# Hash attention and SwiGLU on one core: both query rows of a head pair in sequence, then one stretch of feed-forward work

## The chip, the core and the metric

The kernel runs on one core of one Trainium2 chip. The metric is the device time of one execution in microseconds (us), the median of several runs. A profile of one execution goes with it: the engines are PE (TensorE matmul), PEld (its weight loads), DVE (VectorE), ACT (ScalarE), POOL (GpSimd) and SP (SyncE, which issues transfers).

## The reference

Two blocks follow each other. The attention works on 4 batches of 8 heads, 768 positions of 64 dimensions, with a mask that lets a query see only the keys of its own hash bucket:

```python
q_bits = (np.einsum('bhsd,dk->bhsk', q, proj) > 0)      # 6 bits, the same for k
mask = q_bucket[:, :, :, None] == k_bucket[:, :, None, :]
scores = np.where(mask, scale * np.matmul(q, k.transpose(0, 1, 3, 2)), -1e9)
attn = np.exp(scores - max);  attn = attn / (attn.sum + 1e-9)
x = np.matmul(attn, v)      # heads side by side: 3072 tokens x 512
g = x @ w_gate              # 512 x 1536
out = (g * sigmoid(g) * (x @ w_val)) @ w_out            # 1536 x 512
```

All matrix products are in fp32.

## The kernel before

**Attention.** Heads are taken in pairs, 16 in all (`n` = 0 to 15, four to a batch). For each pair the 768 queries fall into two rows (`half` 0 and 1) of 384; each row runs over 6 blocks of 128 keys (`NCH`). A row's steps are

- `score(u)` (L484): for each key block, fp32 products of q and k for both heads and a bf16 product of hash signs that adds the mask (`sc`, L494); ScalarE takes the exponential into one of six weight buffers (L497);
- `add(u)` (L518): VectorE adds the row's weights of the six key blocks into `acc`, one operation of 128 x 768 for each of the blocks 1 to 5 (L523, L527);
- `attend(u)` (L500): weights times v (`av`, L509), then ScalarE copies the result to `xT`;
- after the second row `total(n)` (L529): four PE products with ones sum `acc` of both rows over the partitions (`sum`, L540), VectorE takes the reciprocal (L548), and eight transfers on SP's queue spread it; `norm` (L558, L560) multiplies `xT` by it later, when `finish(waiting)` comes.

The next pair is prepared by `front(n + 1)` (L388): from pair 5 on two transposes on VectorE (L457), then four small PE products for the hash (`hps`, L412), four sign operations on ScalarE (L417), a transfer that spreads q's signs (L429) and two VectorE operations for k's (L426). `load` (L108) fetches q, k and v of the pair after it, on SP's queue.

**Feed-forward.** A batch whose four pairs are done is pushed by `push_ffn` (L832) as a list of `atoms`, small steps written in PE order: six groups `both(i)` of up products (`up`), then three groups `chunk(i)` of down products (`po`). They use Strassen's scheme, so operands are combined by VectorE (`plus`, L597) before or after the products. In batches 1 to 3 a group of up products is nested: `deeper` (L703) splits two products again, and `weigh` (L696) forms their combined weights, four VectorE operations on 128 x 128. `weigh(0)` of a group can be made ahead by `look_ahead()` (L585), which the last step of the group before calls too. The operands made once for each batch, 16 VectorE operations, stand in the list `first` and are issued by `finish(first)`. A group's steps have sizes that add up to 14. The weights come back from DRAM in pieces: `bring` (L322) issues a transfer on POOL's queue once the product that read the old piece is done.

**Order.** The program order is written out by hand in the loop at L862. From pair 4 on (`gating`) a stretch of feed-forward steps of the batch before follows each row: the loop adds 14 (pairs 4 to 7) or 15.75 (pairs 8 to 15) to `credit` and takes steps until the credit is used up, but only stops at the end of a group. `chores`, one for each unit of size, weave the next pair's preparation into the stretch: in the first row's stretch the two transposes, in the second row's stretch the hash and what follows from it. PE takes its matmuls in this order, and each engine its own instructions.

PSUM has seven rotating banks for all of `sc`, `up`, `po`, `hps` and `sum`, and one for `av`.

Of the kernel before, what the change touches and what calls it, by code (L numbers as in the profile page):

```python
# [18 lines left out]
def kernel(  # L19
# [20 lines left out]
    NP = H // 2  # L40
# [32 lines left out]
    pairs = [(b, pr) for b in range(B) for pr in range(NP)]  # L73
    raws = {}

    def fetch(n, name, queue, half=None):
        b, pr = pairs[n]
        if name == "v":
            t = raws["v", n] = raw.tile([P, 2, NCH, D], FP32, tag="vraw", name="vraw")
            queue.dma_start(  # L80
                t.rearrange("p h c d -> p h (c d)"),
                v[b, 2 * pr : 2 * pr + 2].rearrange("h (p c) d -> p h (c d)", c=NCH),
            )
            return
        src = q if name == "q" else k
        if not half:
            raws[name, n] = raw.tile([P, NCH, 2, D], FP32, tag=name + "raw", name=name + "raw",
                                     bufs=1)
        t = raws[name, n]
        if n <= NP:  # L90
            cs = slice(None) if half is None else slice(half * CH, (half + 1) * CH)
            for h in range(2):
                queue.dma_start(t[:, cs, h, :],
                                src[b, 2 * pr + h].rearrange("(p c) d -> p c d", c=NCH)[:, cs, :])
            return


        blocks = t.rearrange("p c a b -> p (c a b)").rearrange(
            "p (c a d) -> p c a d", a=P // BLOCK, d=BLOCK)
        for h in range(2):  # L100
            for x in range(D // BLOCK):
                at = h * D + x * BLOCK
                queue.dma_start(
                    blocks[at : at + BLOCK],
                    src[b, 2 * pr + h][:, x * BLOCK : (x + 1) * BLOCK].rearrange(
                        "(a p c) d -> p c a d", c=NCH, p=BLOCK))

    def load(n, names):  # L108
        if n < len(pairs):
            for name in names:  # L110
                fetch(n, name, nc.sync)
# [189 lines left out]
    def scale_ahead():  # L301
        scale_to(min(progress["piece"] + 4, progress["scaled"] + 1))
# [70 lines left out]
    def prepare_on(n):  # L373
        for _ in range(n):
            next(preparing, None)
# [108 lines left out]
    def score(u):  # L484
        n, half, c = units[u]
        qs = slice(half * HQ, (half + 1) * HQ)
        ks = slice(c * P, (c + 1) * P)
        sc = [bank("sc")[:, 0:HQ] for _ in range(2)]
        for x, start in ((T, True), (bits, False)):
            if u < 2 and not start:  # L490
                prepare_pair(1)
            for h in range(2):
                rows = slice(h * D, (h + 1) * D)
                nc.tensor.matmul(sc[h], x["k", n][rows, ks], x["q", n][rows, qs],  # L494
                                 start=start, stop=not start)
        for h in range(2):
            nc.scalar.activation(weights(u)[:, h, 0:HQ], sc[h], AF.Exp,  # L497
                                 scale=SCALE * (OFF / 2 if n <= NP else 1.0))
# [19 lines left out]
    def add(u):  # L518
        n, half, c = units[u]
        a = weights(u)  # L520
        if c == 1:
            acc[n, half] = att.tile([P, 2, HQ], FP32, tag="acc", name="acc")
            nc.vector.scalar_tensor_tensor(out=acc[n, half], in0=weights(u - 1)[:, :, 0:HQ],  # L523
                                           scalar=S * EPS / P, in1=a[:, :, 0:HQ],
                                           op0=ALU.add, op1=ALU.add)
        elif c > 1:
            nc.vector.tensor_tensor(acc[n, half], acc[n, half], a[:, :, 0:HQ], op=ALU.add)  # L527

    def total(n):  # L529

        b, pr = pairs[n]

        ps = av_ps.tile([P, 512], FP32, tag="av", name="sum") if b == 0 else bank("sum")
        t = [acc.pop((n, half)) for half in range(2)]
        for h in range(2):
            for half in range(2):
                g = (2 * h + half) * BLOCK
                nc.tensor.matmul(ps[g : g + BLOCK, 0:HQ], ones, t[half][:, h, :],  # L540
                                 start=True, stop=True)
        if b == 0:
            space = wo.rearrange("p f m -> p (f m)")
            space = space[:, n % 2 * 3 * HQ : (n % 2 + 1) * 3 * HQ].rearrange("p (x q) -> p x q", q=HQ)
            r, t = space[:, 2, :], space[:, 0:2, :]
        else:
            r, t = t[1][:, 0, :], t[0]
        nc.vector.reciprocal(r, ps[:, 0:HQ])  # L548
        for half in range(2):
            for h in range(2):  # L550
                g = (2 * h + half) * BLOCK
                for at in (h * D, h * D + BLOCK):
                    nc.sync.dma_start(t[at : at + BLOCK, half, :], r[g : g + BLOCK, :])
        waiting.append(lambda: norm(n, t))
        if pr == NP - 1:
            push_ffn(b)
# [24 lines left out]
    def finish(todo):  # L581
        while todo:
            todo.pop(0)()

    def look_ahead():  # L585

        if atoms:
            finish(getattr(atoms[0][1], "ahead", []))
# [265 lines left out]
    def prepare_pair(count):  # L854
        for _ in range(count):
            rest.extend(f for f in steps.pop(0)() or [] if f)
# [4 lines left out]
    credit = 0.0  # L861
    for u in range(0, N, NCH):  # L862
        n, half, _ = units[u]
        gating = u >= LATE
        if u == MOVE:
            progress["late"] = True
            for t in late_ring:
                nc.gpsimd.memset(t[:, :, HQ:AW], 1.0)
        for c in range(NCH):
            score(u + c)  # L870
            if u + c == 2 or not gating and half == 1 and c == 2:
                prepare_pair(1)
            if c == 1 and half == 0 and 0 < n <= NP:
                total(n - 1)
            if c:
                add(u + c)
        if n >= 2 * NP:
            look_ahead()
        if (n < NP and half == 1) or u == LATE or (n >= 2 * NP and half == 0):
            finish(waiting)  # L880
        finish(rest)
        if not gating and half == 0:
            steps = front(n + 1)
        if not gating and half == 0 and u > 0:
            prepare_pair(2)
        for _ in range(1 if u else 2):
            scale_ahead()
        for c in range(NCH):
            attend(u + c)
        if not gating:  # L890
            scale_ahead()
        if half == 1:
            load(n + 2, "qkv" if n + 2 > NP else "v")
        elif not gating:
            prepare_pair(2 if u > 0 else 4)
            if n + 2 <= NP:
                load(n + 2, "qk")
        finish(first)
        prepare_on(0 if u == LATE else 4)
        chores = []  # L900
        if half == 1 and n >= NP:
            total(n)
            if n + 1 < len(pairs):
                chores = [None] + steps.pop(0)()
        prepare_on(0 if LATE - NCH <= u <= LATE else 3 if gating or not half else 1)
        if not gating:
            continue
        if n + 1 < len(pairs) and half == 0:
            steps = front(n + 1)
            chores = [None, steps.pop(0), None, steps.pop(0)]  # L910

        credit += 14 if n < 2 * NP else 15.75
        end = True
        part = 0
        while atoms and (credit > 0 or not end):
            size, atom, end = atoms.pop(0)
            credit -= size
            atom()
            part += size
            if n < 2 * NP and part >= 11 or u + NCH == N and part >= 6:  # L920
                finish(waiting)
                if u + NCH == N:
                    finish([first.pop(0) for _ in range(min(2, len(first)))])
            if 5 < part < 14 if u == LATE else part < (9 if u < LATE + 3 * NCH else 11):
                prepare_on(size)
            if 6 < part < 11 or u == LATE and part > 10:
                scale_ahead()
            for _ in range(size):
                if chores:
                    step = chores.pop(0)  # L930
                    chores.extend(step and step() or [])
        while chores:
            step = chores.pop(0)
            chores.extend(step and step() or [])
# [34 lines left out]
```

## Time and profile before

| what | value |
|---|---|
| time, median of 3 runs | 986.15 us (985.97 to 986.3) |
| the profiled execution | 985.97 us |
| its span, first to last instruction | 983.9 us |
| granted TensorE clock | 0.999 |
| first scores of pair 8 | 323.87 us from the span's start |
| one row, first `sc` to the end of `av` | 9.09 us |
| one group of up products (nested) | 17.68 us |
| one group of down products | 18.33 us |
| end of the last `sum` (pair 15) | 784.2 us |

Busy time is the share of the span in which an engine executes; matmuls are pipelined, so starts, and not durations, tell what one costs. The chain that ended last is followed back from the last instruction, at each step to what released it or to the instruction before it on its engine. In a timeline each line is a start, a duration (of all the merged instructions), the engine, its line in the kernel, the operation, output<-inputs and a count; idle time before it and what ended it stand in brackets.

From 323.87 us on, two groups follow the first row of pairs 8 and 12 (the last down group of one batch and the first up group of the next), and one group follows each other row of pairs 8 to 14. In each of those stretches ScalarE and VectorE are busy for part of the time only: in the up group from 461.35 to 479.03 us VectorE for 11.27 us of 17.68.

### The profile page before, as it was taken

To read this page: it belongs to the slowest core of one execution; us is meant where nothing else is said; L and a number is where in the kernel's file an instruction comes from. 1 tells how busy PE (TensorE), PEld (TensorE's weight loads), DVE (VectorE), ACT (ScalarE), POOL (GpSimd) and SP (SyncE) were. 2 spreads that over 40 slices of the span, in tenths; PEclk is the share of its full clock that TensorE was granted. 3 is DMA by queue.
4 is the path that set the end of the run, shared out by engine and by line. 5 is a ranking of instruction groups with operands and counts; after the bars stand their busy time and mean duration, and the time that the engine had idled before them with its cause. 6 is when DMAs were issued, how large, how long until landed. Compare 5 with 4: busy or idle time off the path is not lost.

```text
span 983.9 us, 13575 instructions
## 1 busy us (share of the span) xinstructions
PE 977.7 (99%) x4813; PEld 624.2 (63%) x4813; DVE 669.6 (68%) x1276; ACT 408.2 (41%) x921; POOL 127.2 (13%) x248
## 2 busy tenths in 40 slices
PE   9999999999999999999999999999999999999998
PEld 4444555555576776556567776666556687666787
DVE  5899888888974647768775465676767444767721
ACT  6999555566413225444342224335443212333200
POOL 3232232241100011101110001110101000121000
PEclk9999999999999999999999999999999999999999
DMA  7787685976303043323432204343122011333000
GB/s 231 219 259 220 153 260 171 242 271 172 110 17 78 17 100 106 86 85 93 109 93 45 66 17 113 93 98 103 58 67 76 22 38 65 107 102 110 18 28 33
DMA packets 119987, 107.02 MB, mean 109 GB/s; under 512 B 90032, under 2 KB 104848, under 8 KB 119920
## 3 DMA queue, kind: packets, MB, share of 16 engines
q0 software_dynamic: 18336, 73.29, 23.0%
q1 hardware_dynamic: 100784, 32.67, 14.2%
q8 instruction: 38, 0.62, 0.3%
q10 hardware_dynamic: 800, 0.20, 0.1%
q14 instruction: 29, 0.24, 0.1%
HBM read 81.79 MB, written 17.30 MB: 101 GB/s over the span
## 4 chain that ended last, share of the span: by engine, by line
PE 95%; DVE 2%; ACT 2%; issue 1%; DVEq 0%; ACTq 0%
PE up L593 42%; PE po L593 22%; PE sc L494 15%; PE av L509 12%; PE sum L540 1%; PE hps L412 1%; PE tps L396 1%; ACT A L497 1%; ACT kb L417 1%; DVE room L368 0%; PE idle L134 0%; DVE acc L527 0%; ACT room L497 0%; DVE hid L575 0%; DVE c L571 0%
## 5 line engine op out<-in xcount | busy, mean ns | idle before, releaser
L593 PE MATMUL up<-xT,room 128*128 128x384 f32 (+1 forms) x732 | 243.0, 465 | 0.0
L593 PEld LDWEIGHTS up<-xT,room 128*128 128x128 f32 x732 | 134.8, 190 | 73.3 <-issue 9.8
L593 PE MATMUL up<-xc,room 128*128 128x384 f32 (+1 forms) x540 | 176.9, 455 | 0.0
L327 POOL DMA_DIRECT2D room<-ram x144 | 77.6, 542 | 671.0 <-PE up L593 654.3
L494 PE MATMUL sc<-qT,kT 64*128 64x384 f32 x768 | 159.5, 493 | 0.0
L527 DVE TENSOR_TENSOR acc<-acc,A 128x768 f32<-128x768 f32 x128 | 122.6, 958 | 15.7 <-ACT A L497 2.9
L597 DVE TENSOR_TENSOR c<-c,up 128x192 f32<-128x192 f32 (+1 forms) x198 | 78.8, 406 | 76.7 <-PE up L593 72.3
L593 PEld LDWEIGHTS up<-xc,room 128*128 128x128 f32 x540 | 99.3, 190 | 43.8 <-DVE c L597 1.1
L570 ACT ACTIVATE th<-c 128x384 f32<-128x384 f32 x90 | 47.0, 522 | 156.4 <-DVE c L571 87.6
L497 ACT ACTIVATE A<-sc 128x384 f32<-128x384 f32 x256 | 104.0, 527 | 0.6 <-PE sc L494 0.5
L815 ACT COPY words<-po 128x256 f32<-128x256 f32 x48 | 17.9, 372 | 198.5 <-PE po L593 179.6
L494 PEld LDWEIGHTS sc<-qT,kT 64*128 64x128 f32 x768 | 66.1, 186 | 53.6 <-issue 41.2
L597 DVE TENSOR_TENSOR hid<-hid,up 128x192 f32<-128x192 f32 (+1 forms) x162 | 67.6, 418 | 42.8 <-PE up L593 41.0
L509 PE MATMUL av<-A,vraw 128*64 128x384 f32 (+1 forms) x512 | 88.2, 486 | 0.0
L597 DVE TENSOR_TENSOR words<-words,po 128x256 f32<-128x256 f32 x36 | 15.1, 420 | 95.8 <-PE po L593 95.8
L679 ACT COPY c<-up 128x384 f32<-128x384 f32 x72 | 34.4, 478 | 81.6 <-PE up L593 81.6
L593 PE MATMUL po<-wo,room 128*128 128x256 f32 x288 | 66.3, 379 | 0.5 <-DVE room L597 0.5
L593 PE MATMUL po<-wo,hid 128*128 128x256 f32 x288 | 66.7, 382 | 0.0
L593 PE MATMUL po<-room,hid 128*128 128x256 f32 x288 | 66.2, 379 | 0.5 <-ACT words L815 0.5
L509 PEld LDWEIGHTS av<-A,vraw 128*64 128x64 f32 x512 | 36.7, 137 | 46.0 <-issue 44.4
L494 PE MATMUL sc<-qb,kb 64*128 64x384 bf16 x384 | 63.2, 323 | 0.5 <-DVE kb L426 0.5
L593 PEld LDWEIGHTS po<-wo,hid 128*128 128x128 f32 x288 | 54.1, 190 | 12.1 <-issue 4.9
(137 smaller groups left out, 1166.1 us busy)
## 6 DMA issues: line engine op xcount, KB each, us to landing
room<-ram POOLq DMA_DIRECT2D x96, 384.0 KB, 3.7
vraw<-in_v_dram SPq DMA_DIRECT2D x16, 384.0 KB, 3.3
ram<-room POOLq DMA_DIRECT2D x12, 512.0 KB, 5.0
room<-ram POOLq DMA_DIRECT2D x48, 128.0 KB, 3.5
out_dram<-words SPq DMA_DIRECT2D x48, 128.0 KB, 1.7
room<-in_moe_w_out_dram POOLq DMA_DIRECT2D x10, 512.0 KB, 6.6
qraw<-in_q_dram SPq DMA_DIRECT2D x48, 96.0 KB, 3.0
hid<-in_moe_w_gate_dram POOLq DMA_DIRECT2D x9, 512.0 KB, 6.9
```

What stands on the lines that cost most here:

```text
L327: nc.gpsimd.dma_start(places[k % 2][:, PARTS[go], :], ram[k % NG][:, PARTS[go], :])
L396: nc.tensor.transpose(ps[:, i * P : (i + 1) * P], raws[name, n][:, half * CH + i, :, :].rearrange("p h d -> p (h d)"), ident)
L412: nc.tensor.matmul(tile_[i * BLOCK : (i + 1) * BLOCK, 0:HQ], hash_w, T[name, n][:, half * HQ : (half + 1) * HQ], start=True, stop=True)
L494: nc.tensor.matmul(sc[h], x["k", n][rows, ks], x["q", n][rows, qs], start=start, stop=not start)
L497: nc.scalar.activation(weights(u)[:, h, 0:HQ], sc[h], AF.Exp, scale=SCALE * (OFF / 2 if n <= NP else 1.0))
L509: nc.tensor.matmul(ps[h * D : (h + 1) * D, 0:width], raws["v", n][:, h, c, :], a[:, h, 0:width], start=c == 0, stop=c == NCH - 1)
L527: nc.vector.tensor_tensor(acc[n, half], acc[n, half], a[:, :, 0:HQ], op=ALU.add)
L570: nc.scalar.activation(th, g, AF.Tanh, scale=0.5)
L593: nc.tensor.matmul(ps, a, x, start=start and i == 0, stop=i == len(pairs_) - 1, skip_group_check=True)
L597: nc.vector.tensor_tensor(o, a, b, op=op)
L679: nc.scalar.copy(tile_of(g, spot), c)
L815: nc.scalar.copy(o, c)
```

## The change

For the pairs of the third and fourth batch (`whole`, n >= 8) both rows run one after the other, and one stretch of feed-forward steps follows the second, with a credit of 31.5 in place of twice 15.75. The number of steps taken by the end of a pair is the same. In that stretch stand, in order: the reciprocal and spreading of the pair's sums; at unit 6 and 8 the two transposes, at unit 9 the loads for pair n + 2 (before: behind the second row, ahead of the sum), and at unit 15 the hash, followed by the signs. `look_ahead()` is called only after the second row's scores. `finish(waiting)`, the normalisation of the pair before, and `finish(first)` stay behind the first row. Nothing is changed for pairs 0 to 7, and no instruction is added or removed other than in the order.

```diff
+        whole = n >= 2 * NP
...
-        if n >= 2 * NP:
+        if whole and half:
             look_ahead()
...
-        if half == 1:
+        if whole:
+            pass
+        elif half == 1:
             load(n + 2, "qkv" if n + 2 > NP else "v")
...
         if half == 1 and n >= NP:
             total(n)
-            if n + 1 < len(pairs):
+            if n + 1 < len(pairs) and not whole:
                 chores = [None] + steps.pop(0)()
...
-        if not gating:
+        if not gating or whole and not half:
             continue
-        if n + 1 < len(pairs) and half == 0:
+        if n + 1 < len(pairs) and whole:
+            turn_q, turn_k, hashes = front(n + 1)
+            chores = 5 * [None] + [turn_q, None, turn_k, lambda: load(n + 2, "qkv")]
+            chores += 5 * [None] + [hashes]
+        elif n + 1 < len(pairs) and half == 0:
             steps = front(n + 1)
             chores = [None, steps.pop(0), None, steps.pop(0)]
 
-        credit += 14 if n < 2 * NP else 15.75
+        credit += 31.5 if whole else 14
```

By the order of groups this gives: pair 8, the last down group of batch 0 and up groups 1 and 2 of batch 1; pair 9, up groups 3 and 4; pair 10, up groups 5 and 6; pair 11, down groups 1 and 2; and the same again for pairs 12 to 15. The last down group of batch 2 and all of batch 3 follow after pair 15, as before.

## The prediction

> **What bounds the kernel now.** I read the page's engine rows first, then the chain that ended last in order of time, then single engines' timelines around one pair of heads, then the engines' instruction orders in the two programs.
>
> ```profile
> PE 977.7 (99%) x4813; PEld 624.2 (63%) x4813; DVE 669.6 (68%) x1276; ACT 408.2 (41%) x921; POOL 127.2 (13%) x248
> PE 95%; DVE 2%; ACT 2%; issue 1%; DVEq 0%; ACTq 0%
> ```
>
> The chain names TensorE (PE) for 95% of the span, so only what lengthens or shortens PE's own sequence counts. In the changed region (pairs 8 to 15, from 323.9 us) the chain holds nothing but PE pieces, end to end:
>
> ```profile
> 452.27 5.04 PE sc L494 x36
> 457.31 4.04 PE av L509 x24
> 461.35 17.68 PE up L593 x68
> 479.03 5.04 PE sc L494 x36
> 484.08 4.02 PE av L509 x24
> 488.10 0.94 PE sum L540 x8
> 489.04 0.65 PE hps L412 x8
> 489.69 17.68 PE up L593 x68
> 507.37 5.04 PE sc L494 x36
> ```
>
> That is pair 10: first row (sc, av), a group of up products, second row, the sum of the weights, the hash of the next pair, a second group. The change issues the same matmuls in another order. It can save only switches between kinds of matmul and short waits, and it can lose wherever VectorE (DVE), 68% busy, now comes late. One short wait shows already: sum takes 0.94 here but 0.78 in pair 11 (543.85), with hps 0.65 in both. VectorE's last addition before this sum starts at 484.00 in a run of four lasting 4.14, so it ends at 488.14, while the sum's matmuls start at 488.03: **0.16 us of waiting**, in pairs 8, 9, 10, 12, 13 and 14.
>
> **Part 1, the switches.** Streaming costs come from starts that follow each other without a change of kind: 0.3225 us for a 384-wide fp32 matmul instruction (four in 1.29), 0.1613 for 192-wide, half of it for two that share the array. What a start lies behind these is the switch. The rows of one switch after another, in PE's timeline:
>
> ```profile
> 477.58 1.45 PE L593 MATMUL up<-xT,room 128*128 128x384 f32 x4
> 478.96 0.92 PE L494 MATMUL sc<-qT,kT 64*128 64x384 f32 x4
> 479.71 0.33 PE L494 MATMUL sc<-qb,kb 64*128 64x384 bf16 x2
> 479.87 0.81 PE L494 MATMUL sc<-qT,kT 64*128 64x384 f32 x4
> 480.52 0.33 PE L494 MATMUL sc<-qb,kb 64*128 64x384 bf16 x2
> ```
>
> 477.58 + 1.29 = 478.87, and sc starts at 478.96: 0.09. The first four sc take 0.75, the next four 0.65: 0.10 more. So up to sc costs 0.19. In the same way: av to up 0.10, and 0.11 in the first up run (3.01 from start to start where 2.90 is streaming), 0.21; sum to po with no hash between (783.45 to 784.23, 0.645 streaming) 0.13 + 0.11 = 0.24; sum, hps, po (543.78 to 545.20, 1.29 streaming) again 0.24; av to sc (first heads, 97.06) 0.10 + 0.10 = 0.20. A hash in the middle of other work shows at 89.64: 0.10 to enter, 0.78 for 0.645 of streaming, then the slower first run.
>
> Old order per pair: up to sc 0.19, av to up 0.21, sum, hps, up 0.24: 0.64. New order: av to sc 0.20, sum to up 0.24, and the hash, which now stands after the second group's first step, 0.09 + 0.13 + 0.11 = 0.33: 0.77. That is +0.13 in each of pairs 8 to 14, about +0.9. Pair 15 has no hash and saves 0.20. The waits at the sum go in six pairs: -1.0. **Part 1 comes to -0.3 us**, between -1.7 (a hash inside the group costs only its streaming and the leaving switch is free) and +0.9 (it costs 0.17 more each time, twice the leaving row).
>
> The Trainium skill, TensorEngine Tiling, Key Properties, says that a change of tiling mode drains the array. The starts above agree that a change of kind costs time. Counted by that rule, the new order has one change more per pair with a hash and one fewer in pair 15, six more in all; at an estimated 0.1 to 0.2 each that would be +0.6 to +1.2 before the waits, close to the sum from rows.
>
> **Part 2, VectorE at the head of a batch (pairs 8 and 12).** Here sixteen operand combinations for the batch's up products are due, from the list that is emptied after the first row. In the old program they fall under a gated stretch that begins with po. In VectorE's order of the new program they stand between the additions of the first row and those of the second, and the sum waits for the latter. Pair 12, VectorE's timeline:
>
> ```profile
> 566.41 0.96 DVE L523 SCALAR_TENSOR_TENSOR acc<-room 128x768 f32<-128x768 f32 x1 [4.94 <-ACT room L497]
> 567.48 4.14 DVE L527 TENSOR_TENSOR acc<-acc,A 128x768 f32<-128x768 f32 x4
> 571.54 1.01 DVE L560 SCALAR_TENSOR_TENSOR xT<-xT,e,acc 128x768 f32<-128x768 f32 x1
> 572.47 1.02 DVE L597 TENSOR_TENSOR xc<-xT 128x384 f32<-128x384 f32 x2
> ...
> 579.11 1.02 DVE L597 TENSOR_TENSOR room<-hid,room 128x384 f32<-128x384 f32 x2
> ```
>
> The row's first sc is at 563.53. Additions run 566.41 to 571.62 (5.21), the normalisation follows, and the sixteen take 572.47 to 579.11, 6.64 us, so VectorE is free 15.58 after the row began. The second row's additions then end at 15.58 + 5.21 = 20.79, +0.05 to the matmul. PE gets to the second sum matmul at 5.05 + 4.04 + 5.05 + 4.02 = 18.16, +0.01. **Pair 12 waits 2.67 us.** Pair 8 has its normalisation earlier (321.77): additions end at 331.97, the sixteen at 338.53, 14.66 after the first sc at 323.87; 14.66 + 5.21 + 0.05 - 18.17 = **1.75 us**. Nothing can cover it: PE takes its matmuls in order and sum stands directly before the group. Both ends: none, if the additions could pass the sixteen (the order excludes it); 6.64 each, if all sixteen were exposed. I take 1.75 and 2.67, **+4.4 us**. The following work is not late: the group's first VectorE operand comes more than 8 us after the sum.
>
> The Trainium skill, TensorE: Matmul & The Clock Gate, Part 1, says PE's clock halves after an idle window of about 3.4 us. The longest gap here (0.48 us, at 280.61) left the granted clock at 1.00, and no longer one is shown. By the rule 2.67 is below the window, though close; were it crossed, an estimated 3.4 us at half speed would add 1.7 each time.
>
> **Part 3, other moves, taken at 0.** (a) Two groups now follow each other without attention. VectorE's last pieces of a group end at 482.94, 4.07 after PE's streaming of it ends at 478.87; the next group wants r1 of the first inner product at 2.90 and VectorE has it at 481.42, 2.55; VectorE then starts the next group's sums 0.9 late, but the accumulator they free is wanted 0.4 later still. Six such seams with 0.3 to 0.4 in hand; if the cover fails, up to 0.9 each, the lateness itself. (b) Weights: the last transfer of a group is issued at 479.33 and lands in 3.5 (4.3 at most), at 483.6; VectorE reads it 7.6 after the group's start, 486.5. (c) Pairs 11 and 15: the reciprocal (2.56) stands before the s1 combination; ready 4.0 after the sum, wanted at 4.8 because the first three slices are made earlier. This is the kind of wait seen as 0.48 at 280.61, its price if the cover goes. (d) Loads of q, k, v move behind the transposes on SP's queue: nine issues, about 6.7 us; the out transfers queued behind them are of buffers rewritten a whole group (18.3) later, the spreading of q is issued later in any case, and the loaded data is wanted more than 40 us later. POOL's order does not change. (e) ScalarE: 12 exponentials in 4.8 against 9.1 of PE per row; the second row's buffers were read by additions over by 9.1 at the latest (10.0 is when the first exponential can start). (f) The look-ahead call left out after a first row finds nothing to issue in either program.
>
> **Sum.** 985.97 (span 983.9 and 2.07 around it) - 0.3 + 4.4 = 990.1; the median shown is 986.15, 0.18 above the profiled execution, so **990.2**.
>
> **Rivals.** *Lateness carried from group to group*: the seams of 3a and the s1 of 3c fail. For: VectorE is behind by 4 us at each end of a group and attention no longer lets it catch up. Against: the hand-computed reserves. Up to 6 x 0.9 + 2 x 0.48 = 6.4, typically half: 993.4; chance 0.12. *Faster*: the removed round trip from av to up and back to sc decides. It applies if the sums of pairs 8 and 12 do not wait at all; then per pair 0.20 is saved, 1.6 over eight, the six waits give 1.0, and a hash inside the group must cost no more than beside the sum: 986.15 - 2.6 = 983.5; it is on this side of the bound from a hash below 0.08. Against it stands VectorE's order; chance 0.05. *The change does nothing measurable*: VectorE's sixteen are mostly hidden and switches balance, 986 to 988; chance 0.09. The forecast, 988.6 to 992, has 0.74.
>
> Differences within 0.2% (1.97 us) can't be told from none here. Faster 0.05; same 0.10, a little of the forecast's lower edge with it; slower 0.85. Range 988.2 to 994.0.
>
> **What would show it.** PE waiting for acc before sum at pairs 8 and 12 only, near 1.75 and 2.67; no wait at the other sums; up runs of 35 us without a gap; hps after a group's first four up instructions. Wrong if PE waits at the seams, or if sum comes on time in pairs 8 and 12.

## The result and the profile after

| | before | after |
|---|---|---|
| time, median | 986.06 us (985.76 to 986.30, 4 runs) | 989.68 us (989.58 to 989.87, 4 runs) |
| the profiled execution | 985.97 us | 989.78 us |
| its span | 983.9 us | 988.0 us |

The ratio is 1.0037, 95% interval 1.0020 to 1.0054: slower by 3.6 us. The forecast was 990.2.

The page's engine row and the chain's shares, of the changed kernel:

```profile
PE 978.8 (99%) x4813; PEld 621.7 (63%) x4813; DVE 669.3 (68%) x1276; ACT 409.7 (41%) x921; POOL 127.2 (13%) x248
PE 90%; DVE 6%; ACT 2%; issue 2%; POOL 0%; DMA 0%; DVEq 0%; ACTq 0%; POOLq 0%
```

Every engine executes as many instructions as before, and VectorE is busy no longer (669.6 us before, 669.3 now), but VectorE's share of the chain has risen from 2% to 6%. The busy row of PE still says 99%, so it is the chain that shows where to look. In order of time, first the undisturbed part (the end of pair 9's stretch, then all of pair 10):

```profile
453.89 5.05 PE sc L494 x36
458.94 4.04 PE av L509 x24
462.98 5.05 PE sc L494 x36
468.02 4.02 PE av L509 x24
472.05 0.78 PE sum L540 x8
472.83 18.97 PE up L593 x72
491.80 0.78 PE hps L412 x8
492.58 16.39 PE up L593 x64
508.97 5.04 PE sc L494 x36
```

Two rows, the sum, two groups with the hash inside: all PE, end to end. The sum takes 0.78 and not 0.94, so its wait of 0.16 is gone. From 318 us on, VectorE enters the chain only in pairs 8 and 12. The waits of PE in the same kernel from 318 us on (who waited for whom: us in total, times, longest):

```profile
PE sum L540 <- DVE acc L527: 2.7, 2, 1.8
PE po L593 <- ACT words L815: 0.5, 1, 0.5
```

The second is in the last down groups and stands in the kernel before as well. The first is counted from the modelled ends of the first two sum matmuls, which run ahead of the wait; in an undisturbed pair all eight run together, so the starts give the full price. Pair 8, then pair 12, in PE's timeline:

```profile
341.93 0.83 PE L540 MATMUL sum<-acc,ones 128*32 128x384 f32 x2
343.69 0.85 PE L540 MATMUL sum<-acc,ones 128*32 128x384 f32 x6 [0.93 <-DVE acc L527]
...
583.42 0.83 PE L540 MATMUL sum<-acc,ones 128*32 128x384 f32 x2
586.05 0.85 PE L540 MATMUL sum<-acc,ones 128*32 128x384 f32 x6 [1.79 <-DVE acc L527]
```

Less the 0.01 that these starts lie apart in any case, 1.75 and 2.62 us, against 1.75 and 2.67 forecast. VectorE's timeline in pair 12 shows the queue behind it:

```profile
568.09 0.96 DVE L523 SCALAR_TENSOR_TENSOR acc<-room 128x768 f32<-128x768 f32 x1 [4.88 <-ACT room L497]
569.15 4.14 DVE L527 TENSOR_TENSOR acc<-acc,A 128x768 f32<-128x768 f32 x4
573.22 1.01 DVE L560 SCALAR_TENSOR_TENSOR xT<-xT,e,acc 128x768 f32<-128x768 f32 x1
574.15 1.02 DVE L597 TENSOR_TENSOR xc<-xT 128x384 f32<-128x384 f32 x2
...
580.79 0.95 DVE L523 SCALAR_TENSOR_TENSOR acc<-room 128x768 f32<-128x768 f32 x1
581.85 4.14 DVE L527 TENSOR_TENSOR acc<-acc,A 128x768 f32<-128x768 f32 x4
```

The combinations start at 574.15 and hold the second row's additions until 580.79; these have no wait of their own in brackets, so VectorE works without a pause and they wait for their turn in its order. They end at 585.99, and the sum goes on at 586.05. By stages: from pair 8's first score to pair 12's, 239.66 us before and 241.49 after, +1.83; from there to the end 420.3 and 422.7, +2.4; ahead of pair 8, -0.1. The three make the 4.1 by which the span grew.

### The profile page after: what moved, and what is told of

It reads as the page before. It is cut to its first block, busy times and chain, and to the rows that moved or that the text cites. A ratio compares the mean times of both kernels' runs of the same rounds, so it can differ in the third digit from the quotient of the medians.

```text
span 988.0 us, 13667 instructions
## 1 busy us (share of the span) xinstructions
PE 978.8 (99%) x4813; PEld 621.7 (63%) x4813; DVE 669.3 (68%) x1276; ACT 409.7 (41%) x921; POOL 127.2 (13%) x248
## 4 chain that ended last, share of the span: by engine, by line
PE 90%; DVE 6%; ACT 2%; issue 2%; POOL 0%; DMA 0%; DVEq 0%; ACTq 0%; POOLq 0%
PE up L593 42%; PE po L593 22%; PE sc L494 13%; PE av L509 10%; DVE acc L527 2%; PE sum L540 1%; PE hps L412 1%; ACT A L497 1%; DVE xc L597 1%; PE tps L396 1%; DVE room L368 0%; ACT room L497 0%; PE idle L134 0%; DMA room<-ram 0%; DVE acc L523 0%
```

## The experiments

All kernels compute the reference in full. Their times stand against the kernel before, run beside them on the same chip.

**1. The combinations behind the second row.**

```diff
-        finish(first)
+        if not whole or half:
+            finish(first)
```

> The changed kernel, but the sixteen operand combinations at the head of a batch are issued behind the second row instead of between the rows; nothing else moves. Theory 1 (the sums of pairs 8 and 12 wait for VectorE, 1.75 + 2.62 us in the trace of the changed kernel, and nothing else costs): 989.7 - 4.4 = 985.3 us, and no PE wait before any sum. Theory 2 (the loss is spread over the doubled stretches, groups that follow each other without attention): it stays near 989, as those stretches are untouched. Theory 3 (the combinations are merely moved and the down group after them then waits for VectorE): 987 to 989, with new PE waits in the po group of pairs 8 and 12.

Measured: 985.44 us beside 985.87, ratio 0.9995 (0.9987 to 1.0004). The sums of pairs 8 and 12 in PE's timeline:

```profile
341.85 0.85 PE L540 MATMUL sum<-acc,ones 128*32 128x384 f32 x8
342.63 2.86 PE L593 MATMUL po<-wo,hid 128*128 128x256 f32 x12
...
581.59 0.85 PE L540 MATMUL sum<-acc,ones 128*32 128x384 f32 x8
582.37 2.86 PE L593 MATMUL po<-wo,hid 128*128 128x256 f32 x12
```

Both run through in 0.78; PE waits for VectorE before no sum, and the down groups after them run without a gap too. So moving 16 instructions on VectorE takes back all of the 3.6 us lost, and what is left of the change (-0.43) can't be told from nothing. Theories 2 and 3 fall.

**2. Twelve of the sixteen between the rows.**

```diff
-        finish(first)
+        finish(first if half or not whole else [first.pop(0) for _ in range(min(12, len(first)))])
```

> The changed kernel with twelve of the sixteen combinations between the rows and the last four behind the second row. These four take 1.45 us in the trace (579.34 to 580.79). Theory 1 with a plain sum on VectorE: each of the two waits shrinks by 1.45, to 0.30 and 1.17 us, so 989.7 - 2.9 = 986.8 us. If the waits at the sum are no plain queue on VectorE but come from something released once (a buffer, a transfer): no change from 989.7, or all of the 4.4 gone.

Measured: 987.05 us beside 985.87, ratio 1.0012 (1.0003 to 1.0021). PE's timeline has pair 8's sum to po in 1.09 where experiment 1 has 0.78 (0.31 more), and in pair 12 the sum goes on after 1.18, less the 0.01 as above 1.17:

```profile
342.38 1.15 PE L540 MATMUL sum<-acc,ones 128*32 128x384 f32 x8
343.47 2.86 PE L593 MATMUL po<-wo,hid 128*128 128x256 f32 x12
...
582.43 0.83 PE L540 MATMUL sum<-acc,ones 128*32 128x384 f32 x2
583.61 0.85 PE L540 MATMUL sum<-acc,ones 128*32 128x384 f32 x6 [0.35 <-DVE acc L527]
```

The waits shrink by 1.44 and 1.45, and what was taken out from between the rows lasts 1.45: a plain queue.

**3. Pairs 8 and 12 as before, the other six changed.**

```diff
-        whole = n >= 2 * NP
+        whole = n >= 2 * NP and n % NP > 0
...
-        credit += 31.5 if whole else 14
+        credit += 31.5 if whole else 14 if n < 2 * NP else 15.75
```

> Pairs 8 and 12 as in the kernel before (a stretch after each row), the other six pairs as in the changed kernel. Theory 1: the loss sits in pairs 8 and 12 alone; what is left of the change are the switches of pairs 9 to 11 and 13 to 15 (four times -0.03, +0.13, -0.20 = -0.2): 986.06 - 0.2 = 985.9 us. Theory 2 (a loss in every doubled stretch, 3.6 / 8 a pair): 986.06 + 6 x 0.45 = 988.8 us.

Measured: 985.71 us beside 985.87, ratio 1.0000 (0.9991 to 1.0009). Six doubled stretches cost nothing that can be told from none, so the loss was in the two heads of a batch.

**4. The hash beside the sum again.** On top of experiment 1. The next pair's transposes move too, to between the rows, and the loads for pair n + 2 stand behind the second row again, ahead of the sum:

```diff
-        if whole:
-            pass
+        if whole and not half:
+            if n + 1 < len(pairs):
+                steps = front(n + 1)
+                steps.pop(0)()
+                steps.pop(0)()
         elif half == 1:
             load(n + 2, "qkv" if n + 2 > NP else "v")
...
-            if n + 1 < len(pairs) and not whole:
+            if n + 1 < len(pairs):
                 chores = [None] + steps.pop(0)()
...
-        if n + 1 < len(pairs) and whole:
-            turn_q, turn_k, hashes = front(n + 1)
-            chores = 5 * [None] + [turn_q, None, turn_k, lambda: load(n + 2, "qkv")]
-            chores += 5 * [None] + [hashes]
-        elif n + 1 < len(pairs) and half == 0:
+        if n + 1 < len(pairs) and half == 0:
```

> As e1_combos_after_rows, and the next pair's transposes are made after the first row and its hash stands directly behind the sum, as in the kernel before, so that PE changes kind once less in each of pairs 8 to 14. By the switches read from starts (0.33 for a hash inside a group, of which 0.13 over a hash beside the sum once the group's own start is counted): 7 x 0.09 to 7 x 0.24, so 0.6 to 1.7 us below e1, near 984.4 us if e1 gives 985.3. If a hash inside a group costs only its streaming: the same as e1. If VectorE is late again at a sum through the two transposes (1.9 us between the rows): up to 0.1 a pair above that.

Measured: **983.13 us** beside 985.87, ratio 0.9972 (0.9962 to 0.9983): faster than both kernels, and 2.31 below experiment 1, more than expected. The chain of pair 10 in this kernel:

```profile
451.50 5.05 PE sc L494 x36
456.55 4.04 PE av L509 x24
460.59 5.05 PE sc L494 x36
465.63 4.02 PE av L509 x24
469.65 0.78 PE sum L540 x8
470.44 0.65 PE hps L412 x8
471.08 35.16 PE up L593 x136
506.25 5.05 PE sc L494 x36
```

From the sum's start to the end of the second group 36.60 us; in the changed kernel 36.92 (472.05 to 508.97). The 0.32 times seven hashes is 2.2. That PE waits in neither stretch leaves the place of the hash, and not the loads or the transposes, as what differs. My expectation of 0.09 to 0.24 a pair was a slip of arithmetic: the rows of the prediction had said that a hash beside the sum adds nothing to the switch (0.24 with it and without it), so that the whole 0.33 of a hash inside a group goes, 7 x 0.33 = 2.3. VectorE's two transposes between the rows (461.46 to 463.29) delay nothing: the second row's additions begin at 463.40, 2.88 behind the row's first score, as they do in the row of pair 12 before (563.53 to 566.41), where no transpose stands ahead of them.

**5. Combinations and transposes both between the rows.** Experiment 4 without the edit of experiment 1.

> As e4_hash_by_sum (next pair's transposes between the rows, hash behind the sum), but with the sixteen combinations between the rows again, as in the changed kernel. Theory 1, a plain queue on VectorE: the waits of the sums of pairs 8 and 12 are those of the changed kernel plus two transposes (1.85 us): 3.6 and 4.5 us, together 8.1 over e4: 983.1 + 8.1 = 991.2 us; no wait in the other pairs, where VectorE's transposes end before the second row's weights are there. It also makes the longest PE gaps of this kernel. If TensorE's granted clock falls after such a gap, as the Trainium skill (TensorE: Matmul & The Clock Gate, Part 1) states for an idle window of about 3.4 us, the profile shows a clock below 1.00 behind a gap; an estimate from that page is up to 1.7 us more each time, 993 to 995 us.

Measured: 993.98 us, six runs from 991.37 to 995.28, beside 986.02; ratio 1.0079 (1.0066 to 1.0091). The waits are near the 3.6 and 4.5 expected: 345.94 - 342.46 = 3.48 in pair 8, 588.69 - 584.34 = 4.35 in pair 12, and the run of 991.37 is close to the plain queue's 991.2. The rest goes with the clock. PE's timeline at the two gaps, and behind the longer one:

```profile
342.46 0.83 PE L540 MATMUL sum<-acc,ones 128*32 128x384 f32 x2
345.94 0.52 PE L540 MATMUL sum<-acc,ones 128*32 128x384 f32 x3 [2.64 <-DVE acc L527]
...
584.34 0.83 PE L540 MATMUL sum<-acc,ones 128*32 128x384 f32 x2
588.69 0.52 PE L540 MATMUL sum<-acc,ones 128*32 128x384 f32 x3 [3.51 <-DVE acc L527]
...
590.28 4.33 PE L593 MATMUL po<-wo,hid 128*128 128x256 f32 x12
594.44 2.75 PE L593 MATMUL po<-wo,room 128*128 128x256 f32 x12
```

Twelve matmuls take 4.16 us from start to start; in pair 8 of the same execution they take 2.70 (347.36 to 350.06). The stages of 10 us (span; PE, PEld, DVE, ACT, POOL busy; granted clock; DMA) say why:

```profile
350.00:360.00 10.00, 10.00 (x49) 8.79 (x48) 1.54 (x4) 3.30 (x7) 0.00 (x0) 1.00 0.22 59
580.00:590.00 10.00, 6.49 (x44) 2.17 (x40) 8.39 (x16) 1.77 (x5) 0.00 (x0) 0.99 0.44 89
590.00:600.00 10.00, 10.00 (x41) 8.39 (x39) 3.05 (x3) 2.53 (x6) 0.00 (x0) 0.84 0.18 44
```

0.84 behind pair 12's gap, 1.00 behind pair 8's. Over the six runs the mean granted clock goes from 1.000 (991.37 us) to 0.995 (995.06 and 995.28 us), and the longer runs are those with the lower clock. Only one of the six was profiled, so that the others lost their time at the same place is not shown.

**6. No look-ahead at the ends of groups.** The changed kernel with one call less:

```diff
                 if at == len(todo) - 1:
-                    look_ahead()
                     settle(at + NB)
```

> The changed kernel without the look-ahead in the last step of a group: the weights' sums of the next group (four operations, 1.1 us) are made at its first step, behind the last gate operations of the old group (about 1.5 us). It takes the reserve of the seams away. From the timeline of the seam in pair 8 (group ends at 381.17, its r1 is wanted 2.90 later at 384.07, VectorE would have it near 385.3): 1.3 us of PE wait at the two seams without a hash and the five behind pair 15, and 0.3 at the four seams where the hash gives 1.0 more: 9 + 1.2, so 989.7 + 10 = about 1000 us (996 to 1001). If the seams had a large reserve, contrary to the prediction's 0.3 to 0.4: 989.7, unchanged.

Measured: 1001.58 us beside 986.02, ratio 1.0156 (1.0143 to 1.0170); 11.9 above the changed kernel. PE's timeline at the seam of pair 8, then of pair 9, whose hash stands in the seam:

```profile
380.05 4.36 PE L593 MATMUL up<-xT,room 128*128 128x384 f32 x14
385.55 0.59 PE L593 MATMUL up<-xT,inner 128*128 128x192 f32 x2 [1.15 <-DVE inner L597]
...
439.01 1.88 PE L593 MATMUL up<-xT,room 128*128 128x384 f32 x6
441.07 0.59 PE L593 MATMUL up<-xT,inner 128*128 128x192 f32 x2 [0.17 <-DVE inner L597]
```

Without a wait these starts lie 4.19 and 1.72 apart (379.88 to 384.07 and 437.43 to 439.15 in the changed kernel); here they lie 5.50 and 2.06 apart: 1.31 and 0.34 us. Seven seams of the first kind and four of the second make 10.5 of the 11.9. Another 0.1 at each of the eleven is in the matmuls just behind the wait: the next pair of them starts 0.43 later (385.55 to 385.98), where it is 0.33 without a wait (384.07 to 384.40 in the changed kernel). Together that is 11.6. One VectorE block of 1.1 us in the other order is worth three times the whole change.

## Why the prediction was right, step by step

- **What bounds it**: right. The chain of the changed region is PE's sequence, broken by VectorE in pairs 8 and 12 alone; the busy times of VectorE, ScalarE and GpSimd moved by less than 2 us.
- **Part 1, switches, -0.3**: right as far as it can be told. Experiment 1 leaves this part alone, and its span is 983.5 against 983.9, -0.4; the medians say -0.43, within the noise of none. The traces tell more: from pair 10's first score to pair 11's it is 55.10 us before (452.27 to 507.37) and 55.08 after (453.89 to 508.97), -0.02 where 0.13 - 0.16 = -0.03 was forecast. The terms stood too: a hash inside a group costs 0.32 over one beside the sum (0.33 forecast, from 0.09 + 0.13 + 0.11), and the sum's wait of 0.16 is gone. The count by changes of tiling mode, which drain the array by the Trainium skill (TensorEngine Tiling, Key Properties), at the prediction's estimated 0.1 to 0.2 each, was of the right size as well: +0.6 to +1.2 before the waits, where experiment 1's spans give about +0.6 (-0.4 with 1.0 of waits gone). But only the starts could price a hash inside a group.
- **Part 2, the heads of batches, +4.4**: right in place, mechanism and size, 1.75 and 2.62 against 1.75 and 2.67. Experiments 1 and 2 are the proof: the wait vanishes with the combinations, and shrinks by what is taken out of them.
- **Part 3, nothing from the rest**: right. No wait at any seam, at the po groups of pairs 11 and 15, or for weights. That the reserve at the seams was as small as claimed is shown by experiment 6: VectorE's third operation on the weights, r1, ends at 385.50 there and at 383.71 in the changed kernel, 1.62 later when the group's own 0.17 is taken off, and PE loses 1.31, so about 0.3 was in hand. For (f), the look-ahead call, there is no run of its own; by the order of groups the step behind each first row belongs to a down group, or to an up group whose weights the group before has made ahead.
- **The sum**: 990.2 against 989.68. The span came to the forecast's 988.0. What lies around the span was carried over as 2.07 and is 1.78 in the profiled execution after; the median was put 0.18 above that execution and came 0.10 below it. These two, and not a step, make the half microsecond. Why the first differs I did not find out.
- **The rivals.** Lateness carried over did not occur. The fast rival needed two conditions, no wait in pairs 8 and 12 and a hash that costs no more than beside the sum, and gave 983.5; experiment 4 made both true, and measured 983.13. The change as made meets neither.
- **The clock rule of the Trainium skill** (TensorE: Matmul & The Clock Gate, Part 1: about 3.4 us of idle window halves PE's clock): the prediction set the wait of 2.67 against it, but two of the sum's matmuls run in that time. PE's idle time in the changed kernel's longest gap is 1.79, further below the window than the prediction thought, and its granted clock is 1.00. In experiment 5 the gap of 3.48 holds 2.64 us of idle time and left the clock at 1.00; the one of 4.35 holds 3.51 and brought it down. Both agree with the rule. The first 12 matmuls then ran 1.46 us longer, near the 1.7 that the prediction estimated from it. (The gap of 0.48 was not the longest of the kernel before: PE waits 0.54 us at 14.02 and 1.32 ahead of its first matmul. Nothing in the sum rests on that.)

## What to carry to other kernels

When two stretches of work are merged, ask what the old gap gave to an engine that is off the critical path: here VectorE's batch preparation had lain under a long PE stretch and came to stand in front of a sum that PE waits for. An engine that is 68% busy has room, but its queue has an order; a block of instructions with a late due time must not stand ahead of one with an early one. Price a reordering from starts in the timeline, switch by switch, and put small matmuls of a narrow shape beside others of that shape.

## What the runs showed of the hardware

A gap of 4.35 us between starts on PE, 3.51 us of it idle, cost more than itself: the granted clock in the 10 us around the work that followed (590 to 600) was 0.84. The runs of that kernel scattered over 3.9 us; those of the kernel before, beside it, over 1.9, and of each other kernel here over less than 1. Four 32-column matmuls of the hash cost nothing but their streaming behind the sum, which has the same shape (0.65 us), and 0.32 us more inside a stretch of full-width ones.
